# Lightning attention feeding a SwiGLU block: the last two attention groups attended in one visit, and loads moved past transposes

## The chip, the cores and the metric

The kernel runs on one core of a Trainium2 chip. The metric is the device time of one execution in microseconds (us); lower is better. TensorE's clock was granted in full (1.000) during the profiled execution.

## The reference

Attention with a decaying state runs over q, k, v of 4 batches x 8 heads x 768 positions x 64 channels. Its output, laid out as 3072 tokens x 512, goes through a gated FFN with 1536 hidden columns. Cut to what matters:

```python
for b in range(nb):                                    # blocks of 64 positions
    intra = einsum(qb, kb) * Dmask                     # lam ** (i - j) for i >= j
    intra = einsum(intra, vb)
    inter = einsum(qb * lam_pow, kv_state)
    out[:, :, sl] = intra + inter
    kv_state = lam_block * kv_state + einsum(kb * rev_pow, vb)
x = out.transpose(0, 2, 1, 3).reshape(B * S, H * D)
g = x @ w_gate
return (g * sigmoid(g) * (x @ w_val)) @ w_out
```

## The kernel before

**Groups and tiles.** A group is 256 positions of one batch, all heads; there are 12 groups (0 to 11), three for each batch. Two groups make one FFN tile of 512 tokens, so there are six tiles t = 0 to 5, and tile t takes groups 2t and 2t + 1. Groups 0 to 5 are loaded with two neighbouring positions in a row (512 bytes at a time); groups 6 to 11 are loaded in another layout, with 64 channels in a row (256 bytes), by four DMAs each for k and q and two for v (`load_fp32`, L94; issues at L100 and L107). All loads are issued by SP, in the order of the program.

**The life of a group.** `load_group` (L248) loads k, q, v in float32. `cast_scaled` (L260) casts k on ACT (L263) and scales and casts q on DVE, for group 3 on GpSimd (L265), and then calls `dma_transpose` (L253), which issues on SP a DMA that transposes both into the tile `qkt` (L256). `v_scale` (L240) scales v into `v_s` (L243), on GpSimd. `upd_mm` (L371, matmuls at L387) multiplies k by v: the products for the state. `upd_copy` (L395) copies them out of PSUM on ACT (L401, L409). `state` (L415) adds them up on GpSimd and casts the partial states that `inter` reads (L426 to L437). `scores` (L313; `scores_n`, L345, for groups from 6 on) multiplies q by k (L331, L357) and puts the masking multiply on DVE (L338, L362) into the list `later`, from which `run_later` takes it. `core_a` (L495) runs `inter` (L466: q by the state) and `guard` (L448: a one-column copy on ACT that the following accumulation waits for). `core_b` (L500) runs `intra` (L479: the masked scores by v) and `evac` (L486: the result is copied out of two PSUM banks into the FFN's input `xt`, L491).

**A visit.** From tile 2 on, `attend(g)` (L564) does one group's attention in one go between two FFN steps: `core_a(g)`, then the products and scores of the next group, g + 1, then `core_b(g)` and `state(g + 1)`. `ahead` (L560) makes the products and scores of group 6. All of these matmuls use 64 x 64 tiles of TensorE, while the FFN uses the whole array. The products of groups 8 to 11 are 24 matmuls, those of earlier groups 32; each other part is 32 for groups from 6 on.

**The FFN.** A step is `ffn_fc(t, fc)` (L540): `ffn_gate` (four matmuls at L519, silu on ACT at L523) and `ffn_val` (four at L534, the gating multiply on DVE at L537). Twelve steps make a tile. `ffn_out(t, b)` (L544) is one output block of 128 tokens: twelve matmuls (L552), a copy on ACT (L554) and a store that ACT issues (L555).

**What sets the order.** It is written by hand: the schedule is manual, each engine runs its instructions in the order of the program. The lists `steps` and `plan` hold the FFN steps and what is done after each (`at(n, fn, ...)`); the loop at L808 goes through them. `s0`, `s1a`, `s1b`, `s2`, `sn` name steps of tile 0, of the two halves of tile 1, of the first half of tile 2, and of the tiles from 2 on. PSUM is a ring of eight banks, `bank()` (L80), and `set_bank` moves its pointer. DMAs share eight semaphores in turn; in the built program a DMA waits until the one that last had its semaphore has landed, and this one may be a store that ACT issues. The pools limit how far ahead a tile can be filled: 10 buffers for raw k, q and weights, 4 for v, 4 for v_s, 3 for the cast qk and 3 for qkt, 2 for the masked scores.

**What the steps of the prediction touch.** The step of tile 0 before the two halves 11a and 11b is `s0[10]`. At 11a stands `upd_core(2)` (L580), with the products, intra and inter of group 2. In tile 1 stands `core_upd(3)` (L592): inter(3), then upd_mm(4), then intra(3). In tile 2 the plan has `ahead(6)` after step 4, `attend(6)` after step 7 and `attend(7)` after step 10; in tiles 3 and 4, `attend` after steps 4 and 10.

Of the kernel before, what the change touches and what calls it, by code (L numbers as in the profile page):

```python
# [9 lines left out]
BF16 = mybir.dt.bfloat16  # L10
# [27 lines left out]
def _body(ctx, tc, nc, q, k, v, lam, moe_w_gate, moe_w_val, moe_w_out, out):  # L38
    B, H, S, D = q.shape
    HP = H // 2  # L40
    BLK = 128
# [6 lines left out]
    NG = NBLK * B // 2  # L48
# [20 lines left out]
    ssb_pool = ctx.enter_context(tc.tile_pool(name="ssb", bufs=2))  # L69
# [8 lines left out]
    ring = [0]  # L78
# [13 lines left out]
    st = {}  # L92
# [214 lines left out]
    later = []  # L307

    def run_later(n):
        for _ in range(min(n, len(later))):  # L310
            later.pop(0)()

    def scores(g, cs=(0, 1), warm=0):  # L313
        if g >= NAT0:
            scores_n(g)
            return
        tt = st[("qkt", g)]
        sp = {(c, h2): bank() for c in cs for h2 in range(2)}
        warm_into(sp[(cs[0], 0)], warm)
        if ("ssb", g) not in st:  # L320
            st[("ssb", g)] = ssb_pool.tile([128, 2, HP, 2, BLK], BF16, name="ssb", tag="ssb")
        ssb = st[("ssb", g)]
        for c in cs:
            for hi in range(2):
                for s in range(2):
                    for b2 in range(2):
                        for h2 in range(2):
                            hp = 2 * c + hi
                            dp = slice(h2 * 64, h2 * 64 + 64)
                            n = (hi * 2 + s) * BLK  # L330
                            nc.tensor.matmul(  # L331
                                sp[(c, h2)][b2 * M:b2 * M + M, n:n + BLK],
                                tt[dp, 0, s, hp, b2 * M:b2 * M + M],
                                tt[dp, 1, :, hp, b2 * M:b2 * M + M],
                                start=True, stop=True, skip_group_check=True)
            for h2 in range(2):
                def do_mask(c=c, h2=h2):
                    nc.vector.tensor_tensor(  # L338
                        out=ssb[:, h2, 2 * c:2 * c + 2].rearrange("p a s n -> p a (s n)"),
                        in0=sp[(c, h2)].rearrange("p (a x) -> p a x", a=2),  # L340
                        in1=bap(causal, [[0, 2], [1, 2 * BLK]]),
                        op=ALU.mult)
                later.append(do_mask)

    def scores_n(g):  # L345
        tt = st[("qkt", g)]
        sp = [bank() for _ in range(2)]
        ssb = ssb_pool.tile([128, 2, HP, 2, BLK], BF16, name="ssb", tag="ssb").rearrange(
            "p a h s n -> p (a h s n)")[:, 0:2 * BLK * H // 2].rearrange("p (a h n) -> p a h n", a=2, h=H)
        st[("ssb", g)] = ssb  # L350
        for hp in range(HP):
            for s in range(2):
                for h2 in range(2):
                    for r in range(2):
                        row, hq = (1 - h2, HP - 1 - hp) if r else (h2, hp)
                        dp, rm = slice(row * 64, row * 64 + 64), slice(r * M, r * M + M)
                        nc.tensor.matmul(sp[h2][rm, (hp * 2 + s) * M:(hp * 2 + s) * M + M],  # L357
                                         tt[dp, 0, s, hq, rm], tt[dp, 1, s, hq, rm],
                                         start=True, stop=True, skip_group_check=True)
        for h2 in range(2):  # L360
            def do_mask(h2=h2):
                nc.vector.tensor_tensor(out=ssb[:, h2], in0=sp[h2].rearrange("p (a x) -> p a x", x=M),  # L362
                                        in1=bap(causaln, [[0, 2 * HP], [1, M]]), op=ALU.mult)
            later.append(do_mask)
# [6 lines left out]
    def upd_mm(g, up=None):  # L371
        b, i = groups[g]
        v_s = st[("vs", g)]
        up = up or [bank() for _ in range(2)]
        started = set()
        for s in range(2):
            for hp in range(HP):
                for r in range(2):
                    if g >= NAT0 and i == NG // B - 1 and 2 * s + r == 3:
                        continue  # L380
                    for h2 in range(2):
                        ps = slice(r * M, r * M + M)
                        h = 2 * hp + h2
                        if g >= NAT0 and r:
                            h = H - 1 - h
                        n = hp + (HP * s if g >= NAT0 else 0)
                        nc.tensor.matmul(up[r][h2 * 64:h2 * 64 + 64, n * D:n * D + D],  # L387
                                         st[("qk", g)][ps, 0, s, h * D:h * D + D],
                                         v_s[ps, 2 * hp + h2, s],
                                         start=(r, h2) not in started, stop=(s == 1 or g >= NAT0),  # L390
                                         skip_group_check=True)
                        started.add((r, h2))
        st[("up", g)] = up

    def upd_copy(g, parts=(0, 1)):  # L395
        b, i = groups[g]
        up = st[("up", g)]
        hd = "p (h d) -> p h d"
        if i == 0 and 0 in parts:
            kv = kv_pool.tile([128, HP, D], BF16, name="kvn", tag="kvn1", bufs=2)  # L400
            nc.scalar.copy(out=kv, in_=up[0][:, 0:HP * D].rearrange(hd, h=HP))  # L401
            st[("kv", g)] = [None, kv]
        if 1 not in parts:
            return
        src = []
        for r in range(2):
            n = HP * D if g < NAT0 or (r == 1 and i == NG // B - 1) else 2 * HP * D
            u = kv_pool.tile([128, 2 * HP * D], FP32, name="ups", tag="ups", bufs=4)
            nc.scalar.copy(out=u[:, 0:n], in_=up[r][:, 0:n])  # L409
            src += [(r, u, HP * D * j) for j in range(n // (HP * D))]  # L410

        st[("ups", g)] = [u[:, o:o + HP * D].rearrange(hd, h=HP)
                          for r, u, o in sorted(src, key=lambda x: (x[2], x[0]))]
# [81 lines left out]
    def core_a(g):  # L495
        st[("op", g)] = [bank() for _ in range(2)]
        inter(g, True)
        guard(g)

    def core_b(g, fns=(nc.scalar.copy, nc.scalar.copy)):  # L500
        run_later(len(later))
        intra(g, False)
        evac(g, fns)
# [60 lines left out]
    def attend(g):  # L564
# [8 lines left out]
        if g + 1 < NG:  # L573
            later[:] = late
            state(g + 1)

    def set_bank(n):
        ring[0] = n

# [22 lines left out]
    SPLIT = (DVEC, ACTC)  # L602
# [105 lines left out]
    def at(n, fn, *a):  # L708
        plan.setdefault(n, []).append((fn, a))
# [22 lines left out]
    at(s0[9], scores, 2)  # L732
    at(s0[9], run_later, 4)
    at(s0["11a"], upd_core, 2, SPLIT)
    at(s0["11b"], cast_scaled, 3, nc.gpsimd)
    at(s0["11b"], v_scale, 3, nc.gpsimd)
    at(s0["11b"], state, 2)
    at(s0["11b"], load_group, 4, "v")

    s1a = [step(1, fc, 0, 2) for fc in range(FC)]  # L740
    s1b = [step(1, fc, 2, 4) for fc in range(FC)]
    at(s1a[3], cast_scaled, 4)
    at(s1a[3], load_group, 5)
    for c in range(0, FC, 2):
        at(s1a[3], wo_piece, c, c + 2)

# [32 lines left out]
    at(s2, run_later, 4)  # L779
    at(s2, ffn_out, 0, 1)  # L780
    at(s2, core_b, 5, SPLIT)
    at(s2, ffn_out, 0, 2)
    at(s2, cast_scaled, 6)
    at(s2, load_group, 7, "v")
    at(s2, v_scale, 6, nc.gpsimd)
    at(s2, ffn_out, 0, 3)

    outs = [(1, b) for b in range(4)]
    for t in range(2, NG // 2):
        sn = [step(t, fc, 2 if t == 2 and fc < NH else 0) for fc in range(FC)]  # L790
        if t == 2:
            at(sn[4], v_scale, 7, nc.gpsimd)
            at(sn[4], ahead, 6)
        for j, g in ((4 if t == 2 else 0, 2 * t + 3), (8 if t == 2 else 6, 2 * t + 4)):
            if g < NG:
                at(sn[j], cast_scaled, g)
                if g + 1 < NG:
                    at(sn[j], load_group, g + 1)
                if g > 7:
                    at(sn[1 + j], v_scale, g, nc.gpsimd)  # L800
        if t + 1 < NG // 2:
            at(sn[7 if t == 2 else 4], attend, 2 * t + 2)
            at(sn[10], attend, 2 * t + 3)
        for n, o in zip((1, 5, 7, 9) if t == 2 else (0, 3, 7, 9), outs):
            at(sn[n], ffn_out, *o)
        outs = [(t, b) for b in range(4)]

    for n, (t, fc, b0, b1) in enumerate(steps):  # L808
        if t >= 1 and t + 1 < NG // 2 and ("xt", t + 1) not in st:
            new_xt(t + 1)  # L810
        ffn_fc(t, fc, b0, b1)
        run_later(pace.get(n, 2 if len(later) > 1 else 1))
        for fn, a in plan.get(n, []):
            fn(*a)
            if fn in (attend, ahead):
                run_later(1)
    run_later(len(later))
    for t, b in outs:
# [29 lines left out]
```

## Time and profile before

| | |
|---|---|
| Median of 13 runs | 228.08 us (227.28 to 230.76) |
| The profiled execution | 228.08 us, of which the profile's span is 226.3 |
| DVE, ACT, GpSimd busy | 92.0, 106.4, 89.2 us |
| DMA | 39.70 MB; 32.58 MB on SP's queue (q1), 6.75 MB on ACT's (q10) |
| Nine transposes | 4.6 us from issue to landing in the median, 3.7 to 7.5 |
| Loads of k and q, 128 KB each | 3.7 us from issue to landing in the median |

Times in a profile are us from the first instruction of the span. PE is TensorE's matmuls (PEld its weight loads), DVE is VectorE, ACT is ScalarE, POOL is GpSimd and SP is SyncE; SPq is SP's sequencer, which issues DMAs. L387 is line 387 of the kernel. In the timeline a row is start, length, engine, line, operation, output<-inputs with shapes, and the number of instructions merged; in brackets stands the idle time of the engine before it and what ended it. In the view of waits the numbers are us in total, how many times, and the longest. The chain is the work that ended last, followed back from the last instruction: start, length, what. The page gives shares of the span by engine for it.

### The profile page before, as it was taken

Reading aid. Unit: us, or ns where it says so; the run is one execution under the profiler, and the core shown is the slowest. Engines: PE = TensorE matmul, PEld = TensorE weight load, DVE = VectorE, ACT = ScalarE, POOL = GpSimd, SP = SyncE. Lnnn points to the kernel's source line nnn. Section 1 sums busy time; section 2 is a strip of 40 time slices with the busy share of each in tenths; the row PEclk is TensorE's granted clock in tenths of the full one; section 3 lists DMA queues with packets and bytes.
Section 4 is the critical chain, followed back from the end, with each engine's and each line's share of the span. In section 5 each row is a group of like instructions: output and inputs, shape, how many; then the busy total and the mean of one; then the engine's idle time right before and its main releaser. Section 6 shows DMA issues by size and latency. Waiting matters only on the chain.

```text
span 226.3 us, 6040 instructions
## 1 busy us (share of the span) xinstructions
PE 219.1 (97%) x2504; PEld 122.6 (54%) x2504; DVE 92.0 (41%) x158; ACT 106.4 (47%) x211; POOL 89.2 (39%) x132
## 2 busy tenths in 40 slices
PE   8899999997999999999999999999999999999994
PEld 4665456886886555554544544544544444444442
DVE  2664348565753711933335262253242123222200
ACT  5888584854553353555454453453433423322321
POOL 6674737709593030799663092192150000000000
PEclk9999999999999999999999999999999999999999
DMA  6999999999997999397888938907101101101122
GB/s 194 346 359 344 368 359 318 231 157 306 403 233 160 240 234 187 92 249 187 207 190 211 223 89 219 238 13 139 49 1 46 49 0 46 46 3 46 46 93 93
DMA packets 88028, 39.70 MB, mean 175 GB/s; under 512 B 57666, under 2 KB 83522, under 8 KB 88002
## 3 DMA queue, kind: packets, MB, share of 16 engines
q1 hardware_dynamic: 83490, 32.58, 57.0%
q10 hardware_dynamic: 4512, 6.75, 8.2%
q8 instruction: 19, 0.31, 0.6%
q14 instruction: 7, 0.06, 0.1%
HBM read 28.31 MB, written 6.29 MB: 153 GB/s over the span
## 4 chain that ended last, share of the span: by engine, by line
PE 86%; DMA 6%; POOL 3%; ACT 2%; DVE 1%; issue 1%; SPq 0%; POOLq 0%; DVEq 0%
PE bank L552 28%; PE bank L519 25%; PE bank L534 24%; DMA qraw<-in_q_dram 3%; DMA v<-in_v_dram 3%; PE bank L479 2%; PE bank L466 2%; POOL v_s L243 2%; PE bank L387 1%; PE bank L131 1%; PE bank L357 1%; POOL qk L265 1%; DVE ssb L338 1%; PE bank L331 1%; ACT qkt L296 1%
## 5 line engine op out<-in xcount | busy, mean ns | idle before, releaser
L537 DVE TENSOR_TENSOR h<-sil,bank 128x512 bf16<-128x512 bf16 (+1 forms) x91 | 51.5, 575 | 102.3 <-PE bank L534 81.2
L519 PE MATMUL bank<-xt,wg_sb 128*128 128x512 bf16 (+1 forms) x364 | 77.2, 335 | 0.0
L534 PE MATMUL bank<-xt,wv_sb 128*128 128x512 bf16 (+1 forms) x364 | 77.1, 335 | 0.0
L523 ACT ACTIVATE sil<-bank 128x512 bf16<-128x512 f32 (+1 forms) x91 | 46.1, 513 | 42.6 <-PE bank L519 37.4
L552 PE MATMUL bank<-wo_sb,h 128*128 128x512 bf16 (+2 forms) x300 | 65.5, 371 | 0.0
L534 PEld LDWEIGHTS <-wv_sb 128*128 128x128 bf16 x364 | 35.4, 98 | 27.1 <-DVE wv_sb L689 0.5
L519 PEld LDWEIGHTS <-wg_sb 128*128 128x128 bf16 x364 | 34.4, 98 | 26.0 <-DVE xt L491 0.2
L552 PEld LDWEIGHTS <-h 128*128 128x128 bf16 x300 | 28.7, 98 | 32.7
L554 ACT COPY osb<-bank 128x512 f32<-128x512 f32 (+1 forms) x24 | 14.0, 582 | 56.0 <-PE bank L552 56.0
L243 POOL TENSOR_TENSOR v_s<-v,dec 128x1024 bf16<-128x1024 f32 (+1 forms) x15 | 23.4, 1570 | 33.8 <-DMA v<-in_v_dram 33.5
L426 POOL TENSOR_TENSOR kvf<-kvs,ups 128x256 f32<-128x256 f32 x8 | 6.8, 850 | 27.3 <-ACT ups L409 25.5
L338 DVE TENSOR_TENSOR ssb<-bank,causal 128x512 bf16<-128x512 f32 x24 | 15.5, 683 | 4.7 <-PE bank L331 4.7
L491 ACT CAST xt<-bank 128x512 bf16<-128x512 f32 x19 | 11.6, 658 | 4.3 <-PE bank L479 3.3
L435 POOL CAST kvn<-kvf 64x256 bf16<-64x256 f32 x24 | 11.6, 483 | 1.5
L426 POOL TENSOR_TENSOR kvf<-kvf,ups 128x256 f32<-128x256 f32 x16 | 11.6, 726 | 0.6
L409 ACT COPY ups<-bank 128x256 f32<-128x256 f32 (+1 forms) x24 | 9.5, 451 | 1.4 <-PE bank L387 1.0
L265 DVE TENSOR_TENSOR qk<-qraw,qdn 128x1024 bf16<-128x1024 f32 x6 | 9.0, 1502 | 2.3 <-DMA qraw<-in_q_dram 2.3
L263 ACT CAST qk<-kraw 128x1024 bf16<-128x1024 f32 x9 | 9.4, 1045 | 0.9 <-ACT osb L554 0.5
L362 DVE TENSOR_TENSOR ssb<-bank,causaln 128x512 bf16<-128x512 f32 x12 | 8.2, 687 | 1.4 <-PE bank L357 1.3
L387 PE MATMUL bank<-v_s,qk 64*64 64x64 bf16 x352 | 5.7, 195 | 1.6 <-POOL v_s L243 1.3
L479 PE MATMUL bank<-ssb,v_s 64*64 64x128 bf16 (+1 forms) x384 | 6.9, 207 | 0.3 <-ACT guard L450 0.3
L479 PEld LDWEIGHTS <-v_s 64*64 64x64 bf16 x384 | 5.5, 105 | 1.3 <-issue 0.7
(67 smaller groups left out, 123.1 us busy)
## 6 DMA issues: line engine op xcount, KB each, us to landing
out_dram<-osb ACTq DMA_DIRECT2D x23, 256.0 KB, 2.5
v<-in_v_dram SPq DMA_DIRECT2D x18, 256.0 KB, 4.6
woraw<-in_moe_w_out_dram SPq DMA_DIRECT2D x6, 512.0 KB, 8.3
kraw<-in_k_dram SPq DMA_DIRECT2D x24, 128.0 KB, 3.7
qraw<-in_q_dram SPq DMA_DIRECT2D x24, 128.0 KB, 3.7
wraw<-in_moe_w_gate_dram SPq DMA_DIRECT2D x5, 512.0 KB, 7.0
wraw<-in_moe_w_val_dram SPq DMA_DIRECT2D x5, 512.0 KB, 8.1
kraw<-in_k_dram SPq DMA_DIRECT2D x4, 512.0 KB, 6.4
```

The source lines that it names most:

```text
L243: eng.tensor_tensor(out=st[("vs", g)][:, h0:h1], in0=st[("v", g)][:, h0:h1].rearrange("p h (s d) -> p h s d", s=2), in1=vfac(g, h0, h1), o ...
L338: nc.vector.tensor_tensor(out=ssb[:, h2, 2 * c:2 * c + 2].rearrange("p a s n -> p a (s n)"), in0=sp[(c, h2)].rearrange("p (a x) -> p a x", ...
L426: nc.gpsimd.tensor_tensor(out=o, in0=f, in1=u, op=ALU.add)
L435: nc.gpsimd.tensor_copy(out=o[64 - h2 * 64:128 - h2 * 64], in_=f[h2 * 64:h2 * 64 + 64])
L479: nc.tensor.matmul(op[r][h2 * 64:h2 * 64 + 64, cols(g, hp, s)], v_s[ps, 2 * hp + h2, s], ssb[ps, h2, hp * 2 + s] if g >= NAT0 else ssb[ps, ...
L491: fns[r](out=xt[:, g % 2, :, r].rearrange("p h (m s) -> p h s m", s=2) if g < NAT0 else xt[:, g % 2, :, :, r * M:r * M + M], in_=op[r].rea ...
L519: nc.tensor.matmul(gp[:, 0:N], wg_sb[:, mc, fs], xt[:, b0 // 2:b1 // 2, mc].rearrange("p g b n -> p g (b n)"), start=(mc == 0), stop=(mc = ...
L523: nc.scalar.activation(sil[:, 0:N], gp[:, 0:N], AF.Silu)
L534: nc.tensor.matmul(vp[:, 0:N], wv_sb[:, mc, fs], xt[:, b0 // 2:b1 // 2, mc].rearrange("p g b n -> p g (b n)"), start=(mc == 0), stop=(mc = ...
L537: nc.vector.tensor_tensor(out=h_sb[:, fc % FH, b0:b1].rearrange("p b n -> p (b n)"), in0=sil[:, 0:N], in1=vp[:, 0:N], op=ALU.mult)
L552: nc.tensor.matmul(ps, st[("h", t, fc // FH)][:, fc % FH, b], wo_sb[:, fc, c0:c1], start=(fc == 0), stop=(fc == FC - 1))
L554: fn(out=osb[:, c0:c1], in_=ps)
```

## The change

The masked scores of groups 10 and 11 share one buffer, since those of a group from 6 on fill half of one. `attend_ahead2(9)` takes the place of `attend(9)`: it makes the products and scores of 10 and of 11 within the visit of group 9, with the bank pointer set by hand, and leaves both states to GpSimd after it. `attend_pair(10)`, after step 8 of tile 4, then does the attention of 10 and 11 together, in place of two visits after steps 4 and 10. Its results are copied out by DVE and ACT, as those of group 9 are, where `attend` copies with ACT alone.

The casts of group 3 and the load of v of group 4 move from 11b to step 10 of tile 0, and k, q of group 5 are loaded at 11b. In the built program their SP order becomes: transpose 3, v of 4, k and q of 5, transpose 4, v of 5. Group 6 is cast before the third output block of tile 0. `v_scale(7)` goes to DVE, one step after `ahead(6)`. Of the later loads, k of 9 comes before transpose 8, k and q of 10 before transpose 9, and k and q of 11 before transpose 10. Groups 10 and 11 are cast after steps 3 and 7 of tile 3, where before they were cast after step 6 of tile 3 and step 0 of tile 4.

```diff
--- before.py
+++ after.py
@@ -345,9 +345,14 @@
     def scores_n(g):
         tt = st[("qkt", g)]
         sp = [bank() for _ in range(2)]
-        ssb = ssb_pool.tile([128, 2, HP, 2, BLK], BF16, name="ssb", tag="ssb").rearrange(
-            "p a h s n -> p (a h s n)")[:, 0:2 * BLK * H // 2].rearrange("p (a h n) -> p a h n", a=2, h=H)
-        st[("ssb", g)] = ssb
+        n = 2 * BLK * H // 2
+        if g == NG - 1:
+            both, o = st[("ssb2", g - 1)], n
+        else:
+            both, o = ssb_pool.tile([128, 2, HP, 2, BLK], BF16, name="ssb", tag="ssb").rearrange(
+                "p a h s n -> p (a h s n)"), 0
+        st[("ssb2", g)] = both
+        ssb = st[("ssb", g)] = both[:, o:o + n].rearrange("p (a h n) -> p a h n", a=2, h=H)
         for hp in range(HP):
             for s in range(2):
                 for h2 in range(2):
@@ -573,6 +578,32 @@
         if g + 1 < NG:
             later[:] = late
             state(g + 1)
+
+    def attend_ahead2(g):
+
+
+        run_later(len(later))
+        b0 = ring[0]
+        core_a(g)
+        upd_mm(g + 1)
+        upd_copy(g + 1)
+        scores(g + 1)
+        run_later(len(later))
+        upd_mm(g + 2)
+        core_b(g, SPLIT)
+        upd_copy(g + 2)
+        set_bank(b0 + 2)
+        scores(g + 2)
+        set_bank(b0 + 4)
+        state(g + 1)
+        state(g + 2)
+
+    def attend_pair(g):
+        run_later(len(later))
+        core_a(g)
+        core_a(g + 1)
+        core_b(g, SPLIT)
+        core_b(g + 1, SPLIT)
 
     def set_bank(n):
         ring[0] = n
@@ -732,15 +763,16 @@
     at(s0[9], scores, 2)
     at(s0[9], run_later, 4)
     at(s0["11a"], upd_core, 2, SPLIT)
-    at(s0["11b"], cast_scaled, 3, nc.gpsimd)
+    at(s0[10], cast_scaled, 3, nc.gpsimd)
+    at(s0[10], load_group, 4, "v")
     at(s0["11b"], v_scale, 3, nc.gpsimd)
     at(s0["11b"], state, 2)
-    at(s0["11b"], load_group, 4, "v")
+    at(s0["11b"], load_group, 5, "kq")
 
     s1a = [step(1, fc, 0, 2) for fc in range(FC)]
     s1b = [step(1, fc, 2, 4) for fc in range(FC)]
     at(s1a[3], cast_scaled, 4)
-    at(s1a[3], load_group, 5)
+    at(s1a[3], load_group, 5, "v")
     for c in range(0, FC, 2):
         at(s1a[3], wo_piece, c, c + 2)
 
@@ -779,28 +811,41 @@
     at(s2, run_later, 4)
     at(s2, ffn_out, 0, 1)
     at(s2, core_b, 5, SPLIT)
-    at(s2, ffn_out, 0, 2)
     at(s2, cast_scaled, 6)
     at(s2, load_group, 7, "v")
     at(s2, v_scale, 6, nc.gpsimd)
+    at(s2, ffn_out, 0, 2)
     at(s2, ffn_out, 0, 3)
 
     outs = [(1, b) for b in range(4)]
     for t in range(2, NG // 2):
         sn = [step(t, fc, 2 if t == 2 and fc < NH else 0) for fc in range(FC)]
         if t == 2:
-            at(sn[4], v_scale, 7, nc.gpsimd)
             at(sn[4], ahead, 6)
-        for j, g in ((4 if t == 2 else 0, 2 * t + 3), (8 if t == 2 else 6, 2 * t + 4)):
-            if g < NG:
-                at(sn[j], cast_scaled, g)
-                if g + 1 < NG:
-                    at(sn[j], load_group, g + 1)
-                if g > 7:
-                    at(sn[1 + j], v_scale, g, nc.gpsimd)
-        if t + 1 < NG // 2:
-            at(sn[7 if t == 2 else 4], attend, 2 * t + 2)
-            at(sn[10], attend, 2 * t + 3)
+            at(sn[4], cast_scaled, 7)
+            at(sn[4], load_group, 8)
+            at(sn[5], v_scale, 7, nc.vector)
+            at(sn[6], load_group, 9, "k")
+            at(sn[7], attend, 6)
+            at(sn[8], cast_scaled, 8)
+            at(sn[8], load_group, 9, "qv")
+            at(sn[9], v_scale, 8, nc.gpsimd)
+            at(sn[10], load_group, 10, "kq")
+            at(sn[10], attend, 7)
+        elif t == 3:
+            at(sn[0], cast_scaled, 9)
+            at(sn[0], load_group, 10, "v")
+            at(sn[0], load_group, 11, "kq")
+            at(sn[1], v_scale, 9, nc.gpsimd)
+            at(sn[3], cast_scaled, 10)
+            at(sn[3], load_group, 11, "v")
+            at(sn[4], attend, 8)
+            at(sn[5], v_scale, 10, nc.gpsimd)
+            at(sn[7], cast_scaled, 11)
+            at(sn[8], v_scale, 11, nc.gpsimd)
+            at(sn[10], attend_ahead2, 9)
+        elif t == 4:
+            at(sn[8], attend_pair, 10)
         for n, o in zip((1, 5, 7, 9) if t == 2 else (0, 3, 7, 9), outs):
             at(sn[n], ffn_out, *o)
         outs = [(t, b) for b in range(4)]
@@ -812,7 +857,7 @@
         run_later(pace.get(n, 2 if len(later) > 1 else 1))
         for fn, a in plan.get(n, []):
             fn(*a)
-            if fn in (attend, ahead):
+            if fn in (attend, ahead, attend_ahead2):
                 run_later(1)
     run_later(len(later))
     for t, b in outs:
```

## The prediction

> **What bounds the kernel now.** I read the page first: its engine row, then the chain that ended last.
>
> ```profile
> span 226.3 us, 6040 instructions
> PE 219.1 (97%) x2504; PEld 122.6 (54%) x2504; DVE 92.0 (41%) x158; ACT 106.4 (47%) x211; POOL 89.2 (39%) x132
> ...
> PE 86%; DMA 6%; POOL 3%; ACT 2%; DVE 1%; issue 1%; SPq 0%; POOLq 0%; DVEq 0%
> ```
>
> TensorE is the bound. No other engine is half busy, and in the chain four matmuls of 512 columns take 0.86 us wherever FFN runs. The change adds and removes no matmul, so it can win only where TensorE idles or crawls: the attention visits. The waits of TensorE alone say where:
>
> ```profile
> PE bank L387 <- POOL v_s L243: 1.3, 1, 1.3
> ...
> PE bank L479 <- ACT guard L450: 0.3, 1, 0.3
> ```
>
> One wait is large. The timeline from 40 to 53 us shows its cause (start, length, engine):
>
> ```profile
> 41.73 2.00 SPq L256 DMA_TRANSPOSE qkt<-qk  x1
> ...
> 43.78 0.56 SPq L100 DMA_DIRECT2D v<-in_v_dram  x1
> 45.44 4.49 SPq L256 DMA_TRANSPOSE qkt<-qk  x1
> ...
> 50.40 1.91 POOL L243 TENSOR_TENSOR v_s<-v,dec 128x1024 bf16<-128x1024 f32 x1 [6.66 <-DMA v<-in_v_dram]
> ...
> 52.37 0.45 PE L387 MATMUL bank<-v_s,qk 64*64 64x64 bf16 x32 [1.31 <-POOL v_s L243]
> ```
>
> SP issues the load of v of group 4 only at 43.78, behind group 3's transpose. It lands 6.5 us later, yet the view of windows has the DMA at 4 GB/s from 48 to 50 us: something held the DMA engines during group 4's transpose. GpSimd scales v from 50.40, and upd_mm(4) waits 1.31 us.
>
> Second, a collision at 91.9 us and where it ends:
>
> ```profile
> 91.87 1.92 POOL L243 TENSOR_TENSOR v_s<-v,dec 128x1024 bf16<-128x1024 f32 x1 [10.70 <-DMA v<-in_v_dram]
> 91.94 2.93 DVE L265 TENSOR_TENSOR qk<-qraw,qdn 128x1024 bf16<-128x1024 f32 x1
> ...
> 93.74 1.71 POOL L426 TENSOR_TENSOR kvf<-kvs,ups 128x256 f32<-128x256 f32 x1
> ```
>
> The DVE cast of group 7 takes 2.93 us against 1.20 to 1.23 elsewhere. state(6) stands behind v_scale(7) on GpSimd, so its last cast (98.38, two of 0.85 in all) ends at 99.23, when inter(6) is already running.
>
> Third, what a visit costs. The chain, cut to 95 to 101 us and then to 140 to 182 us:
>
> ```profile
> 99.13 0.56 PE bank L466 x32
> ...
> 100.42 0.32 PE bank L479 x32
> 100.74 0.32 PE bank L552
> ```
>
> ```profile
> 145.09 0.38 PE bank L466 x32
> ...
> 146.00 0.32 PE bank L479 x32
> 146.32 0.97 PE bank L519 x4
> ```
>
> Visit 9 lasts 145.09 to 146.32, 1.23 us; 10 lasts 1.18 (161.97 to 163.15); 11 lasts 1.09 (178.80 to 179.89) though it has half the matmuls, for it waits 0.23 us on the guard. After each the first four FFN matmuls take 0.97, not 0.86. Visit 6 lasts 1.61.
>
> **What the Trainium skill says.** "SBUF — State Buffer", section "Who interferes with whom": a DVE tensor_tensor with two SBUF inputs and a GpSimd instruction that reads SBUF exclude each other for a whole instruction. The trace agrees (2.93 for 1.20). "Perfetto Trace Analysis", section "DMA Instruction — HWDGE (DVE, Sync)": the shown length of a DMA is issue alone and starts when its semaphores are met. It agrees: v shows 0.56 and lands after 6.5. "DMA: Bandwidth & Descriptors", section "Issuing engines are not separate DMA queues": SP's and ACT's transfers interleave on the same 16 engines. It agrees: one store out issued in the crowded stretch at 83.43 is 6.7 us in landing, where the median is 2.0. "TensorEngine Tiling (Array Packing)", section "Key Properties": a change of tiling mode drains TensorE; 0.97 against 0.86 is what this trace shows of it.
>
> **Part 1: group 3's casts at step 10 instead of 11b, and k, q of group 5 ahead of group 4's transpose.** The k cast on ACT (1.04) now stands before silu of 11a. k lands near 36.5 and the silu before it ends at 36.55, so the cast runs 36.6 to 37.6 and that silu 37.6 to 38.0; the next on ACT, the copy of the state product, began at 38.02 anyway. Cost 0, with 0.1 us to spare; if k lands late, inter(2) waits as much: bounds 0 and +0.5. The q cast on GpSimd waits for its load (38.11 to 40.03) in both. The transpose can issue at 40.05, since ACT no longer ends at 41.66: v is issued near 42.1 instead of 43.78 and lands near 46 to 48, even with a held transpose. v_scale(4) is then done by 50, upd_mm(4) is wanted at 51.06. The wait goes: **-1.31**. What is late next is the guard of group 3 on ACT, which the 0.45 of upd_mm(4) covers. k and q of group 5 then go before 45.44 instead of at 49.98, filling the empty 48 to 50; the wo pieces and transpose 5 follow about 3 us sooner, for no gain: all was hidden. Group 4's transpose now queues behind 1 MB (some 3.4 us at 300 GB/s), landing near 52; scores(4) come at 60.4.
>
> **Part 2: group 6's casts before the third output block of tile 0, v_scale(7) on DVE.** The ACT cast (1.04) falls in a gap of ACT (free from 78.7 to 80.2): 0. v_scale(7) costs DVE 1.2 (its row for the same shape, L265) and frees 1.92 on GpSimd: state(6) starts at 92.2, waits out the DVE cast (91.94 to 93.2), and ends near 97 to 98.7, before inter(6) at 99.06. Visit 6 falls from 1.61 to 1.34 (0.38 inter, 0.33 products, 0.31 scores, 0.32 intra, from visit 9's pieces and a third more products): **-0.27**. DVE's own queue (gating multiplies of 0.69 every 1.73 us, a mask) is late by 1.2 to 2.4; eight PSUM banks, two to a step, cover it. Bounds -0.3 and +0.4.
>
> **Part 3: loads moved past transposes.** In the built order SP has k of group 9 (4 issues of 0.64, 2.6 us) before transpose 8, k and q of 10 before transpose 9, k and q of 11 before transpose 10. Transpose 8 also waits for the DMA semaphore of a store on ACT (tile 1, block 2, issued 104.09 and landed 3.7 us later), and transpose 9 for the store of tile 2, block 0 (issued 119.36). Transpose 8 was issued at 107.88, and with the least landing time of 3.7 us arrives as scores(8) begin at 111.58. Now: transpose 7 issues at 93.3 instead of 95.01, its loads end 1.7 sooner, k of 9 fills 103.1 to 105.8, and the transpose goes at 107.5 as before. Bounds -0.1 and +0.8 for its data standing behind k's; I take **+0.1**. Transpose 9: near 122 instead of 120.60, lands by 126, wanted at 128.6: 0. Groups 10 and 11 land 4 us or more ahead of the joint visit. Silu and stores behind the new ACT casts have TensorE's banks as cover: 0.
>
> **Part 4: the visits.** Before: 1.23 + 1.18 + 1.09 and 3 x 0.11 for the re-entry = 3.83. After: visit 9 gains 24 products and 32 scores: 1.23 + 0.25 + 0.31 = 1.79. The scores of 11 take the two banks that ACT empties of group 10's products: a guard (0.16), then copies of 0.59 and 0.38, ready some 1.8 us into the visit, while TensorE is there at 1.5. Wait 0.3 (bounds 0 and 0.6). The double visit 10, 11: 0.38 + 0.31 + 2 x 0.32 = 1.33, its guards covered by the other group. Two re-entries, 0.22. Sum 3.64: **-0.19**. Its DVE and ACT copies of x are wanted three steps later: 0; after visit 9 DVE has two masks and a copy (2.1 us) before step 0 of the next tile, 0.6 us in time.
>
> **Sum.** 1.31 + 0.27 - 0.1 + 0.19 = 1.67. The profiled execution took 228.08 (span 226.3 and 1.8 around it), which is also the median of the 13 runs; 228.08 - 1.67 = 226.4.
>
> **Rivals.** (B) The v wait is only shortened: the held transpose recurs, or ACT's early cast is late. For it: k's 0.1 us margin. Against: v has 2 to 4 us of slack now. With 0.4 of the 1.31 won: 227.3. (C) Slower: transpose 8 behind k of group 9. Landing times of transposes reach 7.5 us when other transfers are in flight (median 4.6). Price: 107.5 + 7.5 = 115.0 against scores(8) at about 111.3: TensorE stands for 3.7 us, and 226.4 + 3.7 gives 230.1. It decides from 5.9 us of landing on (113.4), where the stall passes 2.1. Against: k is issued early enough to be through at 108. (D) Nothing to be had: the 1.31 returns elsewhere in the chain of loads, as transposes 9 to 11 now wait on stores, and the visits gain nothing: 228.1.
>
> **Chances.** A, the forecast (225.6 to 227.1), 0.68; B 0.16; C 0.09; D 0.07. About 0.2% (0.46 us) is what a measurement of this kernel can tell from no change: faster means under 227.62. A and nearly nine tenths of B lie there: 0.82; D and the rest of B: 0.09; C: 0.09. The range goes from 225.5 (the low bounds together take 0.5 off 226.4; the runs of before scatter 0.8 below their median, of which I allow half) to 228.0, leaving out C, half of D and a little of A.
>
> **What would show it.** Right: no TensorE wait on v_s near 51; v of group 4 issued near 42; the DVE cast of group 7 near 1.3; visit 6 near 1.35; one visit of about 2.1 and one of 1.35 where three were. Wrong: a wait at L331, L357 or L387 (the last two are five lines lower after the edit) on a transpose or v_s, first of all in the visit of group 7; silu 11a delaying inter(2); or a scores-11 wait over 0.6 us.

## The result, and the profile after

The changed kernel takes **229.97 us** in the median of 11 runs (229.02 to 231.51), against 228.08 for the kernel before in the same session: ratio 1.0085, 95% interval 1.006 to 1.011. The forecast was 226.4 us, with 225.5 to 228.0 as its range. The change makes the kernel slower.

The profiled execution spans 228.0 us where before spanned 226.3. The head of its page, the engine row and the row of the chain by engine:

```profile
span 228.0 us, 6039 instructions
PE 219.9 (96%) x2504; PEld 123.1 (54%) x2504; DVE 94.6 (41%) x162; ACT 105.2 (46%) x208; POOL 86.0 (38%) x131
...
PE 83%; DMA 7%; SPq 6%; issue 1%; DVE 1%; ACT 0%; POOL 0%; DVEq 0%; ACTq 0%
```

TensorE has the same number of matmuls and is busy for 0.8 us more in a span that is 1.7 us longer, so it stands still for longer. Its waits (total, times, longest) say where, and what is gone:

```profile
PE bank L362 <- issue: 1.9, 1, 1.9
...
PE bank L484 <- DVE ssb L338: 0.6, 1, 0.6
...
PE bank L471 <- ACT guard L455: 0.3, 1, 0.3
```

The wait for v_s, 1.3 us before, isn't in the list. In its place stand 0.6 us at `intra` (L484) for a mask of DVE, and 1.9 us at `scores_n` (L362) put down to "issue": no semaphore event of another engine explains it. The timeline of TensorE around it (start, length, line, what; in brackets the idle time before it):

```profile
145.87 0.42 PE L484 MATMUL bank<-ssb,v_s 64*64 64x64 bf16 x27
146.17 0.66 PE L362 MATMUL bank<-qkt 64*64 64x64 bf16 x26
148.74 0.25 PE L362 MATMUL bank<-qkt 64*64 64x64 bf16 x6 [1.91 <-issue]
148.92 1.04 PE L524 MATMUL bank<-xt,wg_sb 128*128 128x512 bf16 x4
```

These are the scores of group 11 in the long visit. 26 of 32 matmuls run, then nothing for 1.9 us, then the last six. All 32 read the same tile and write the same two banks, and both banks are already written in the first 26, so neither transpose 11 nor ScalarE's copies out of those banks can be what the last six miss. The view of windows has in the pause (146.9 to 148.7 us) no matmul and no weight load, at full clock, and no transfer that began there. (The row gives the stretch, its length, the busy time of PE, PEld, DVE, ACT and POOL with the number of instructions, the granted clock, and the DMA's share and rate; a transfer counts where it begins.)

```profile
146.90:148.70 1.80, 0.00 (x0) 0.00 (x0) 0.75 (x2) 0.79 (x3) 1.54 (x4) 1.00 0.00 0
```

The view of the DMA from 144.5 to 150 us has the data of a store and two packets of another kind, by queue (packets, MB, share):

```profile
q10 hardware_dynamic: 144, 0.26, 12.3%
q8 instruction: 2, 0.03, 2.8%
```

A queue of its own moves instructions, and over the whole span the page has this row for it:

```profile
q8 instruction: 19, 0.31, 0.6%
```

0.31 MB in 19 packets is 16 KB each. The Trainium skill, "Runtime: NRT & Kernel Launch", section "Instruction fetch mechanics", says that an engine's instructions come in blocks of 16 KiB, 256 instructions, which its sequencer fetches through its own DMA queue while it executes. The trace agrees on the count: TensorE has 2504 matmuls and 2504 weight loads, 5008 / 256 = 19.6, and the run e12 below, whose list is 98 instructions longer, has a 20th packet. The same section calls the cost mostly hidden. Here the packet records have the first of the two packets from 146.11 to 147.45, and TensorE goes on at 148.74, 1.29 us after its end.

Set side by side FFN matmul by FFN matmul, the two traces differ as follows. The start is 0.28 us later (it differs from one execution to the next). In the visit of group 3, 0.45 us is won, not 1.31; in visit 6, 0.17; visits 7 and 8 don't change. The visit of group 9 costs 2.98 us more. Visit 10 gives back 1.29, the pair 10 and 11 costs 1.49, visit 11 gives back 1.20. The end is 1.67 us later.

### The profile page after: what moved, and what is told of

It reads as the page before. It is cut to its first block, busy times and chain, and to the rows that moved or that the text cites. A ratio compares the mean times of both kernels' runs of the same rounds, so it can differ in the third digit from the quotient of the medians.

```text
span 228.0 us, 6039 instructions
## 1 busy us (share of the span) xinstructions
PE 219.9 (96%) x2504; PEld 123.1 (54%) x2504; DVE 94.6 (41%) x162; ACT 105.2 (46%) x208; POOL 86.0 (38%) x131
## 4 chain that ended last, share of the span: by engine, by line
PE 83%; DMA 7%; SPq 6%; issue 1%; DVE 1%; ACT 0%; POOL 0%; DVEq 0%; ACTq 0%
PE bank L557 27%; PE bank L524 24%; PE bank L539 24%; DMA qraw<-in_q_dram 4%; DMA wraw<-in_moe_w_val_dram 3%; SPq L100 3%; SPq L218 3%; PE bank L471 2%; PE bank L484 2%; PE bank L392 1%; PE bank L331 1%; PE bank L362 1%; PE bank L294 1%; ACT ups L414 0%; POOL qk L278 0%
## 5 line engine op out<-in xcount | busy, mean ns | idle before, releaser
L243 POOL TENSOR_TENSOR v_s<-v,dec 128x1024 bf16<-128x1024 f32 (+1 forms) x14 | 21.8, 1563 | 24.9 <-DMA v<-in_v_dram 24.7
L431 POOL TENSOR_TENSOR kvf<-kvs,ups 128x256 f32<-128x256 f32 x8 | 5.8, 727 | 26.8 <-ACT ups L414 15.2
L496 ACT CAST xt<-bank 128x512 bf16<-128x512 f32 x16 | 10.0, 666 | 3.5 <-PE bank L484 2.5
L440 POOL CAST kvn<-kvf 64x256 bf16<-64x256 f32 x24 | 10.4, 433 | 1.5
L265 DVE TENSOR_TENSOR qk<-qraw,qdn 128x1024 bf16<-128x1024 f32 x6 | 8.1, 1350 | 1.7 <-DMA qraw<-in_q_dram 1.7
L484 PE MATMUL bank<-ssb,v_s 64*64 64x128 bf16 (+1 forms) x384 | 6.8, 207 | 0.6 <-DVE ssb L338 0.6
L496 DVE CAST xt<-bank 128x512 bf16<-128x512 f32 x8 | 5.6, 715 | 3.9 <-PE bank L484 3.9
L484 PEld LDWEIGHTS <-v_s 64*64 64x64 bf16 x384 | 5.5, 106 | 1.8 <-issue 1.1
```

Of the source, the lines that this page charges most:

```text
L243: eng.tensor_tensor(out=st[("vs", g)][:, h0:h1], in0=st[("v", g)][:, h0:h1].rearrange("p h (s d) -> p h s d", s=2), in1=vfac(g, h0, h1), o ...
L431: nc.gpsimd.tensor_tensor(out=o, in0=f, in1=u, op=ALU.add)
L440: nc.gpsimd.tensor_copy(out=o[64 - h2 * 64:128 - h2 * 64], in_=f[h2 * 64:h2 * 64 + 64])
L484: nc.tensor.matmul(op[r][h2 * 64:h2 * 64 + 64, cols(g, hp, s)], v_s[ps, 2 * hp + h2, s], ssb[ps, h2, hp * 2 + s] if g >= NAT0 else ssb[ps, ...
L496: fns[r](out=xt[:, g % 2, :, r].rearrange("p h (m s) -> p h s m", s=2) if g < NAT0 else xt[:, g % 2, :, :, r * M:r * M + M], in_=op[r].rea ...
```

## The experiments

My theory after the result: **TensorE runs out of instructions in the long visit.** A 64x64 matmul is two instructions (a weight load and the matmul), which TensorE gets through in about 10 ns together. The visit of group 9 has grown from 120 matmuls to 176, 352 instructions in some 2 us, more than one block. The place in TensorE's list where one block ends and the next begins is called a block edge below. The rivals: the last scores wait for operands or banks, or the moved loads and casts are what costs. The diffs are against the changed kernel where nothing else is said, and "ratio" is always to the kernel before, with the 95% interval.

**e1, visits put back.** The scores of group 11 have a buffer of their own again, which the cut of the diff leaves out.

```diff
-            at(sn[10], attend_ahead2, 9)
+            at(sn[10], attend, 9)
         elif t == 4:
-            at(sn[8], attend_pair, 10)
+            at(sn[4], attend, 10)
+            at(sn[10], attend, 11)
```

> The changed kernel with only the visits put back: group 9 alone, then 10 and 11 in a visit each, as before; the earlier casts and loads and the v_scale of group 7 on VectorE stay. If the loss comes from TensorE running out of instructions in the long visit (my theory), the 1.9 us standstill goes with the visit and what is left are the two gains before it, measured as 0.45 and 0.22 us in the profiles: about 227.4 us, ratio to the kernel before 0.996 to 0.999, and no pause over 0.3 us inside any visit. If the moved loads and casts are what costs (rival), it stays at 229.5 to 230 us, ratio 1.006 or more.

Measured: 228.26 us, ratio 1.0005 (0.9991 to 1.0019), no pause in a visit. The loss is gone with the visits, so the moved loads and casts alone don't make it. But the gain that I expected to be left isn't there either: Parts 1 to 3 of the prediction together bring nothing that can be measured. e9 and e10 below say why.

**e2, scores of group 11 after the next step.**

```diff
         upd_copy(g + 2)
-        set_bank(b0 + 2)
-        scores(g + 2)
         set_bank(b0 + 4)
...
             at(sn[10], attend_ahead2, 9)
+            at(sn[11], scores, 11)
```

> The changed kernel with the scores of group 11 taken out of the long visit and made after the next feed-forward step (same matmuls, banks of the ring as they come). The visit then has 288 TensorE instructions instead of 352, and 16 follow slowly before the 64 of the scores. Instruction theory: the refill has a whole step of 1.7 us more to arrive; the standstill falls from 1.9 to at most 0.3 us, one more change between packed and full matmuls costs about 0.3; 227.8 to 228.5 us, ratio about 1.000. If scores 11 waited for its operands or its banks (ScalarE's two ups copies, transpose 11, v_s of 11), the same wait would be gone too, so this run doesn't tell those apart, but the next two do. If the moved loads cost it: 229.5 to 230.

Measured: 228.06 us, ratio 1.0015 (0.9995 to 1.0036), as expected. The scores run through, in the timeline of TensorE:

```profile
147.21 1.03 PE L539 MATMUL bank<-xt,wv_sb 128*128 128x512 bf16 x4
148.17 0.45 PE L362 MATMUL bank<-qkt 64*64 64x64 bf16 x32
148.54 1.04 PE L524 MATMUL bank<-xt,wg_sb 128*128 128x512 bf16 x4
```

**e3, a shorter list ahead of the visit.** Only the warm-up at the start of the kernel is changed, 140 us before the visit:

```diff
-    for n in range(30):
+    for n in range(7):
...
-    warm_up(4)
+    warm_up(5)
```

> The changed kernel, where only the opening warm-up differs: 23 of the 30 small 64x8 matmuls are left out and one 512-column warm-up is added for about the same time, so TensorE's list is 44 instructions shorter ahead of everything else. Nothing near the long visit is touched. Instruction theory: the block edges lie 44 instructions later in the visit, so the 256-instruction block that was missing at the visit's last 6 matmuls is needed only some 32 instructions after it, two feed-forward steps later, and has come by then: the standstill of 1.9 us goes to under 0.3 us, about 228.0 us, ratio 0.998 to 1.001. Every rival (banks, copies, transpose, moved loads): no change, 229.5 to 230 us with the 1.9 us pause after 26 matmuls of scores 11.

Measured: 227.75 us, ratio 0.9986 (0.9964 to 1.0008), as expected. The pause is gone, with the visit itself untouched:

```profile
146.05 0.42 PE L484 MATMUL bank<-ssb,v_s 64*64 64x64 bf16 x27
146.35 0.71 PE L362 MATMUL bank<-qkt 64*64 64x64 bf16 x32
147.00 1.04 PE L524 MATMUL bank<-xt,wg_sb 128*128 128x512 bf16 x4
```

The visit now costs 0.88 us more than before, not 2.98: the pause was worth 2.10. In the chain it runs from 144.96 to 147.07:

```profile
144.96 0.38 PE bank L471 x32
...
147.07 0.97 PE bank L524 x4
```

A wait of 0.9 us on "issue" is left in e3's list, at L392. It ends at 14.86 us, in the opening, at one of the block edges that the counting below gives; the changed kernel has 0.4 us there.

**e4, a longer list.** The same place, the other way: `range(47)` for `range(30)` and `warm_up(3)` for `warm_up(4)`, 32 instructions more.

> As the run with fewer, the other way: 17 more small matmuls and one 512-column warm-up less in the opening, so TensorE's list is 32 instructions longer. Instruction theory: the edge comes 32 instructions sooner in the visit, so the pause of 1.9 to 2.1 us stays but falls 16 matmuls earlier: after about 10 matmuls of scores 11 instead of 26, with some 22 left behind it; 229.7 to 230.2 us, ratio 1.006 to 1.011. Every rival: the pause stays after 26 of the 32.

Measured: 231.63 us, ratio 1.0159 (1.0132 to 1.0185), slower than I expected. The pause moved by 16 matmuls, from after 26 to after 10:

```profile
147.94 0.53 PE L362 MATMUL bank<-qkt 64*64 64x64 bf16 x10
150.20 0.38 PE L362 MATMUL bank<-qkt 64*64 64x64 bf16 x22 [1.73 <-issue]
```

And a second one appeared where none had been, among slow FFN matmuls two steps after the visit of group 3 (the timeline of TensorE):

```profile
67.98 0.38 PE L524 MATMUL bank<-xt,wg_sb 128*128 128x256 bf16 x2
68.84 0.38 PE L524 MATMUL bank<-xt,wg_sb 128*128 128x256 bf16 x2 [0.47 <-issue]
```

That is one part of what the time was over my number; the larger is a weight cast that TensorE waits for at 20 us (0.9), after the changed opening. Counted along TensorE's list in the trace, the pauses stand at instruction 1985 and 4033 here and at 4033 in the changed kernel. (The weight loads are counted, two instructions to each, since the trace misses a few matmuls of e4.) 4033 - 1985 is 2048, eight blocks of 256. No bank, copy or transpose knows such a distance.

**e5, the visits alone.** The kernel before, with the diff of the long visit and the pair, and of the loads only what they need. In tile 3 that is:

```diff
+            at(sn[0], cast_scaled, 9)
+            at(sn[0], load_group, 10)
+            at(sn[0], load_group, 11, "kq")
...
+            at(sn[3], cast_scaled, 10)
+            at(sn[3], load_group, 11, "v")
```

> The kernel before with the visits alone changed (the long visit of group 9, the pair of 10 and 11), and of the loads only those that this needs; casts of 3 and v of 4, v_scale of 7 as before. TensorE's list has the same length ahead of the visit as in the changed kernel. Instruction theory: the pause of about 2 us stands inside scores 11 after 26 of its matmuls, as in the changed kernel, and without the gains of the earlier part the sum is +2.0 us: 230.0 to 230.5, ratio 1.008 to 1.012. If moved loads or casts made the pause: no pause, 227.8 to 228.1.

Measured: 233.65 us, ratio 1.0218 (1.0182 to 1.0254). The pause is where the theory has it, after 26 of the 32, at instruction 4033 again:

```profile
148.58 0.66 PE L362 MATMUL bank<-qkt 64*64 64x64 bf16 x26
151.08 0.27 PE L362 MATMUL bank<-qkt 64*64 64x64 bf16 x6 [1.85 <-issue]
```

The time is some 3 us over what I expected, and most of that comes from an order of mine. k and q of group 10 were asked for in the same step as 11's, three steps ahead of their cast, and the casts stood at the head of ScalarE and VectorE until they came. The waits from 124 to 134 us:

```profile
DVE qk L265 <- DMA qraw<-in_q_dram: 6.4, 1, 6.4
ACT qk L263 <- DMA kraw<-in_k_dram: 4.3, 1, 4.3
...
PE bank L362 <- ACT osb L559: 0.7, 1, 0.7
```

Side by side with the kernel before, the FFN matmuls lose 2.7 us there, and another 1.6 us just after the pause, where TensorE's clock is at half (in the row of the windows view, the 0.50 ahead of the last two figures):

```profile
151.20:154.50 3.30, 3.30 (x14) 1.22 (x10) 0.69 (x1) 0.60 (x1) 2.97 (x7) 0.50 0.02 5
```

So the long visit needs the earlier loads, and e5 shows the place of the pause but doesn't size the visits.

**e6, the opening of e3 on the kernel before.** A control.

> Control: the kernel before with the opening of the run with fewer small matmuls (23 left out, one 512-column warm-up added) and nothing else. Its visits have at most 256 TensorE instructions. Instruction theory: there is no pause to take away, ratio 0.998 to 1.002. If the shorter opening itself gains (a rival for the gain of the run with fewer): 226 us, ratio 0.990 to 0.994.

Measured: 227.72 us, ratio 0.9989 (0.9969 to 1.0009), as expected. The opening gains nothing by itself that these runs can tell. Next to e3 (227.75) this is also the fairest judgement on the change without its pause: no difference that these runs can tell.

**e7, e3 and an earlier mask.** The second of group 3's masks is made a step sooner:

```diff
-    at(s1a[7], run_later, 1)
+    at(s1a[7], run_later, 2)
```

> The run with fewer small matmuls, and the second of group 3's masks made in step 7 of tile 1, where VectorE idles 0.99 us, instead of after step 8, so that the fourth is done a step sooner. If the pause of 0.87 us in intra 3 is VectorE's fourth mask (theory: it took back half of what the removed v_s wait gave), it falls to under 0.2 us and the time by 0.5 to 0.7: 227.0 to 227.4 us, ratio 0.994 to 0.997. If something else holds that place once the mask is early (v_s of 4, inter 3's copies), the pause stays at some other wait and the time at 227.7.

Measured: 227.23 us, ratio 0.9961 (0.9937 to 0.9985). The time is as expected. But in the profiled execution the mask's wait was followed by another, after all of `intra(3)`:

```profile
51.02 0.64 PE L484 MATMUL bank<-ssb,v_s 64*64 64x128 bf16 x32
53.20 0.60 PE L524 MATMUL bank<-xt,wg_sb 128*128 128x256 bf16 x4 [1.54 <-issue]
```

It stands at instruction 1473 of the list, 2560 ahead of 4033: ten blocks. The wait for the mask had hidden a block edge. Profile and timed runs part ways here: in the profile this visit is 0.7 us longer than in e3, and the median of the runs is 0.5 us shorter. The profiled execution took 227.77 us, itself 0.5 above that median, so how often this pause occurs isn't known.

**e8, e2 and the earlier mask.**

> The run with the scores of group 11 after the next step, with the second mask of group 3 made sooner as in the run before; TensorE's list is as long ahead of the visit as in the changed kernel. Theory: neither the pause in the visit nor that in intra 3, 0.6 us less than 228.06: 227.2 to 227.6, ratio 0.995 to 0.998, and about the same as the run with fewer and the mask. If the mask isn't what holds intra 3: 228.0.

Measured: 227.36 us, ratio 0.9962 (0.9946 to 0.9979). Here too a pause is at 1473, shorter, and inside `intra(3)`, since the list ahead is 44 instructions longer than in e7:

```profile
51.77 0.35 PE L484 MATMUL bank<-ssb,v_s 64*64 64x128 bf16 x10
52.54 0.52 PE L484 MATMUL bank<-ssb,v_s 64*64 64x128 bf16 x22 [0.41 <-issue]
```

22 matmuls are left where e7 had none: 22 x 2 = 44. e7 and e8 are faster than both the kernel before and the changed one.

**e9 and e10, the kernel before profiled again**, for the gain of Part 1 that was missing in e1. e5 and e6 have the casts of group 3 as before, and neither showed a wait for v_s.

> The kernel before once more, for a second profiled execution. The two runs that kept its first half showed v of 4 landing 4.4 to 4.7 us after its issue and no wait for v_s of 4, where the first profile of before has 6.5 us and a wait of 1.31. If that wait belonged to the one execution (an instruction fetch of 1.97 us that fell into the transposes), it's absent here: v of 4 lands at about 48.4 us and the wait in the visit of group 3 is the mask's 0.63. If it belongs to the kernel: 1.3 us for v_s again.

> The kernel before, a third profiled execution, with the same two cases as the run before it: no wait for v_s of 4 and 0.63 us for the mask (the wait was one execution's), or 1.3 us for v_s (the kernel's).

One timed run each, 228.56 and 229.16 us, spans 226.9 and 227.5. Neither has the wait for v_s of the first profile. (e9's list has one of 0.8 us at L387, but for an earlier group, at 14.67 us.) v of group 4 is issued at 44.68 in e9 and lands 4.5 us later (4.2 in e10), where the first profile had 6.5. The timeline of e9, and its waits from 50 to 54.5 us:

```profile
44.68 0.57 SPq L100 DMA_DIRECT2D v<-in_v_dram  x1
...
49.28 1.91 POOL L243 TENSOR_TENSOR v_s<-v,dec 128x1024 bf16<-128x1024 f32 x1 [4.75 <-DMA v<-in_v_dram]
```

```profile
PE bank L479 <- DVE ssb L338: 0.6, 1, 0.6
```

The mask holds the visit of group 3 in both, by 0.6 us, as in the changed kernel. In the first profile an instruction packet of 1.97 us began at 47.42 us, with transposes and v in flight; in e9 one of 1.33 us began at 48.69 and in e10 one of 1.22 at 48.76, when v was nearly in. That this coincidence is what held v is the likeliest reading; no run forced it.

The two also show visit 6 at its worst. In e10 the chain passes through GpSimd's state casts:

```profile
99.87 0.41 POOL kvn L435
100.33 0.40 PE bank L466 x25
```

There visit 6 costs 0.42 us more than in the first profile, 0.46 in e9.

**e11, the kernel before with the earlier mask** and nothing else.

> The kernel before with nothing but the second mask of group 3 made in step 7 of tile 1. If the mask alone brings what the runs with a mask gained (0.5 to 0.7 us), the change's own parts are worth about nothing: 227.4 to 227.6 us, ratio 0.996 to 0.998. If v_s of 4 is what holds the visit of group 3 in the kernel before, the mask brings nothing: ratio 0.999 to 1.001.

Measured: 227.50 us, ratio 0.9974 (0.9952 to 0.9996), as expected. In its profile neither a mask nor the block edge, which lies in `intra(3)`, stops TensorE in the visit of group 3:

```profile
51.20 0.64 PE L479 MATMUL bank<-ssb,v_s 64*64 64x128 bf16 x32
51.77 0.61 PE L519 MATMUL bank<-xt,wg_sb 128*128 128x256 bf16 x4
```

One line on the kernel before gives most of what e7 and e8 have; their intervals overlap.

**e12, a list 98 instructions longer, with the earlier mask**: `range(82)` and `warm_up(1)`.

> The changed kernel with the mask sooner, and 98 more TensorE instructions in the opening (52 small matmuls more, three 512-column warm-ups less). The instruction theory places the block edges from the pauses seen so far (at 1473 and 4033 of the list): 98 instructions more put none of them into the visit of group 3 or the last three quarters of the long visit. It expects no pause over 0.3 us in either: 226.9 to 227.5 us, ratio 0.994 to 0.998, unless the longer opening itself costs (its first matmuls came 0.7 us later in the run with 32 more). If the pauses aren't at fixed edges of the list, there is one of 0.6 us or more in one of the visits.

Measured: 231.99 us, ratio 1.0149 (1.0098 to 1.0200). No pause in either visit, and TensorE's list of waits has "issue" nowhere. But I had placed the edges wrongly: counted in the trace, the one at 1473 lies at the start of the visit of group 3, and the one at 4033 in `intra` of the long visit, at 150.33 us. It stops nothing, because the packet for it had ended at 147.20, before the visit: slow matmuls of an output block stand among the instructions ahead of this edge. So e12 fits the theory of the supply, but isn't the test of the edges' places that I meant it to be. The time was far off, for three reasons. The first FFN matmuls come 2.06 us later than before, and 0.4 of that is left at 54 us. TensorE then waits for a transpose, as in rival C of the prediction:

```profile
PE bank L362 <- DMA qkt<-qk: 2.4, 1, 2.4
```

That is scores(8), in the visit of group 7. An instruction packet at 105.75 us took 1.84 us amid the loads of k of group 9; their last landed at 110.28 instead of 108.78. A store issued at 104.30 landed at 109.19 and let transpose 8 go only at 109.27 (107.79 in the changed kernel), and the transpose took 5.1 us instead of 3.7. Third, right after this wait TensorE's clock is at half:

```profile
114.50:117.80 3.30, 3.30 (x70) 1.76 (x71) 0.69 (x1) 1.51 (x3) 2.59 (x5) 0.50 1.04 237
```

Half the clock for 3.41 us costs up to 1.7 us (an estimate from these two figures). The one of e12's six executions with a mean clock of 0.998 took 229.96 us, the five at 0.992 to 0.993 took 231.8 to 233.3.

## Why the prediction was wrong

**The bound, TensorE, was right**, and so was the reading that only the visits can win or lose.

Two steps failed. The forecast was 3.6 us short of the result; the pause is 2.10 of it, and the 1.31 that Part 1 had to win is nearly all of the rest.

**Part 4 failed in one place: it put the supply of instructions at nothing.** "Visit 9 gains 24 products and 32 scores: 1.23 + 0.25 + 0.31 = 1.79", with 0.3 for ScalarE's copies, 2.1 in all. The work was costed rightly: in e3, from the chain, the visit runs from 144.96 to 147.07, which is 2.11. Over all visits from 9 on, e3 measures 0.88 - 1.29 + 1.49 - 1.20 = -0.12, forecast -0.19. What the sum left out is that 352 instructions have to be there. The pause, 2.10 us, is the whole loss against the kernel before. I listed a wait over 0.6 us at the scores of 11 as a sign of being wrong, but for the copies; the chain has those done at 146.40, when TensorE comes for the banks.

**Part 1 failed at its starting point.** The 1.31 us belonged to the one profiled execution, not to the kernel: e9, e10, e5 and e6 don't have it. The step "v is issued near 42.1 instead of 43.78" failed as well: SP sat 3.51 us in the issue of transpose 3, from 40.32, and v went out at 43.89. And the wait behind, DVE's fourth mask, was not seen: I named the guard as what is late next. The 0.45 that the first pair of traces shows in this visit is just what e9 and e10 show without any change (0.45 in each).

**Part 2 held in the profile.** Visit 6 lasts 1.39 us (99.03 to 100.42 in the chain; forecast 1.34), the DVE cast 1.60 (forecast 1.2 to 1.3). Its worth moves with the execution: 0.17 against the first profile, some 0.6 against e9 and e10. The collision that I started from moves, too: in e9 and e10 the DVE cast of group 7 takes 1.22 us, not 2.93, and `v_scale(7)` holds up state(6) by starting only at 93.38 and 93.90. In the timed runs of e1 no gain of Part 2 can be seen. **Part 3 held in the changed kernel** with no margin: transpose 8 landed at 111.47, and scores(8) began at 111.51. e12, with another opening and mask, shows the other outcome, so rival C was a real danger.

**The rivals.** The sign came from none of them. C had the right size (230.1) with the wrong cause, by luck.

**What stays open.** Two profiled executions of the same visit (e7, e11) have the packet at different times, 50.76 and 48.20 us. About 1 us of this is the list, which is 44 instructions longer in e11; the rest isn't settled, and the order of loads around it differs between the two. Whether a pause brings the half clock that followed it in e5 isn't settled either. Nor can these runs size the change without its pause better than e3 beside e6 does, some 0.3% either way.

## What to carry to other kernels

Count TensorE's instructions, not only its time: a stretch of packed 64x64 matmuls uses two instructions in about 10 ns, and where a stretch of about 300 or more meets a block edge badly, TensorE can stand for 2 us with nothing in the profile but "issue". With loads in flight a shorter one was enough (e7: 144 instructions, 1.54 us). Splitting the stretch with slow matmuls took the pause away in e2. Any instruction added or removed anywhere ahead moves the work against the edges. Before a wait in a profile is counted as a gain, take a second profile of the same kernel, and look for what is late next in the same visit.

## What was unexpected of the hardware

- **The supply of instructions to TensorE can be measured.** The packets can be put in order beside the block edges, which lie 256 instructions apart with 1473, 1985 and 4033 among them (the first packet of the span belongs to the edge at 449). In all fourteen profiles TensorE began no block sooner than 1.25 us after its packet had ended, and the six pauses of this document ended 1.29 to 1.58 us after. The packet itself takes 0.88 us at the least and 2.57 at the most. After the first 30 us, no 294 instructions ahead of an edge passed in less than 3.57 us (the number 294 is fitted to these traces). Where TensorE was quicker and other DMA traffic light, it paused until 3.67, 3.79 and 3.86 us had passed (e4, e5, the changed kernel). With loads and transposes in flight the pauses ended 6.1 to 7.4 us after (e8, e7, the one at 68.84 us in e4). The section of the Trainium skill named above also gives TensorE a store of 2048 instructions. In these traces no packet began more than 298 instructions ahead of its edge, so nothing like 2048 was held ahead, and the measurement decides.
- **TensorE's clock was halved for 3.41 us after some of its waits.** In e12 this began at 114.47 us, 0.03 after a wait of 2.38, and in e5 at 151.18, 0.10 after the pause of 1.85. In the profiles of the changed kernel, e4 and e7 pauses of 1.91, 1.73 and 1.54 us were not followed by it. In the timed runs a mean clock of 0.993 or less stands in 4 of 11 of the changed kernel, 4 of 6 of e5 and 5 of 6 of e12, and in 11 of the 137 runs of the kernel before that were taken beside the experiments. That the waits bring it is likely but not shown: e6, with no such wait in its profile, has it in 4 of 22.
- **An instruction packet and the data beside it were slow together, twice.** e12's packet of 1.84 us went with k landing 1.5 us later than in the changed kernel, and that of 1.97 us in the first profile with v of group 4 landing 6.5 us after its issue. Which of the two held up the other, these traces don't tell.
